# Later steps for the coefficient checks beside attention and for a layer's first normalisations

## The chip, the cores and the metric

The kernel runs on one core of a Trainium2 chip. The metric is the device time of one execution in microseconds (us), lower is better. A core has five engines that work side by side and wait for each other through semaphores: TensorE (PE, matmuls; its weight loads are listed apart as PEld), VectorE (DVE), ScalarE (ACT), GpSimd (POOL) and SyncE (SP), which here issues nearly all transfers between memory and the core. Each engine takes its own instructions strictly in the order in which they were put into its queue. So an instruction that waits holds up everything behind it on that engine, also what would be ready.

## The reference

Two blocks alternate, A B A B, on a sequence of 2048 rows of 512 numbers, each with a layer norm ahead and a residual sum behind. B's weights are the same both times.

```python
def _A_ref(x, dft_seq_re, dft_seq_im, dft_hid_re, dft_hid_im):
    a = jnp.einsum("bsd,ed->bse", x, dft_hid_re)
    b = jnp.einsum("bsd,ed->bse", x, dft_hid_im)
    return jnp.einsum("ts,bse->bte", dft_seq_re, a) - jnp.einsum("ts,bse->bte", dft_seq_im, b)

def _B_ref(x, wq, wk, wv, wo, beta):          # 32 heads of 16, 4 segments of 512 rows
    for s in range(N):
        logits = jnp.einsum("bhqd,bhkd->bhqk", qs, ks) * scale + mask
        a_dot = jnp.einsum("bhqk,bhkd->bhqd", _softmax(logits), vs)
        a_mem = (phi(qs) @ M) / (phi(qs) @ z + 1e-6)
        outs.append(g * a_mem + (1.0 - g) * a_dot)
        M = M + phi(ks).T @ vs; z = z + phi(ks).sum()
    return o @ wo

x = x + _A_ref(_layernorm(x), ...); x = x + _B_ref(_layernorm(x), ...)
x = x + _A_ref(_layernorm(x), ...); x = x + _B_ref(_layernorm(x), ...)
```

## The kernel before, in words

**Two layers.** A layer is a block A, here computed with far fewer matmuls than the reference, and a block B. Block A folds the sequence: rows that a Fourier matrix treats alike up to sign are added or subtracted first, so that a quarter of the matrix is left (`place_folded`). The 2048 rows come as eight octants; `A` and `B` in the code name four of them that belong to the first two segments of the attention before, `C` two of the third, `D` two of the fourth. For each half `k` (0 and 1) of the octants, the generator `fold(k)` goes through steps: load A and B; patch single edge rows (`edge`); normalise A and B (`normalise(k, "AB")`: four statistics on VectorE, one power on GpSimd, some small operations, four scalings on ScalarE); load C, patch it, normalise it; form sums and differences; take in D; fold again. The tile of A and B, `hAB`, lies in the buffer in which attention keeps the transposed rows `xT`, so it can be filled once the fourth segment's projections are done. After the folds, `contract` runs the matmuls with the Fourier coefficients.

**The checks.** Folding is only right if the Fourier matrices that are passed in have the symmetry that it uses. So the kernel reads both whole matrices and checks them, and falls back to a plain program if the check fails. There are 68 check units (`place_checks`), each a transfer of 512 KB into a tile `chk` and one or four ScalarE instructions that form the absolute differences and their sum (L900). Units 0 to 33 belong to the first layer and 34 to 67 to the second. Of each 34, the first 20 run beside the folds and the contraction, and the other 14 beside attention, one every 15 steps from step 85 of the attention on.

**Attention.** There are 4 segments x 4 groups x 2 = 32 units a layer, each of four heads, and a unit starts every ten steps. In its ten steps TensorE computes transposed scores `sT`, one piece a step; ScalarE clears what the mask forbids and takes the exponential into a probability tile `pT` (L1171, L1172); two steps behind the ten, a block of 32 matmuls (`pv_bank`) multiplies the probabilities with the values, and ScalarE copies the result to `ot` (L1245). Beside this run, for later units, the row maxima on VectorE (`nat`, `junk`, L1098), and for other segments projections, transposes, memory and output projection. The last two groups of the fourth segment apply the mask with a matmul, so there ScalarE has no clearing and GpSimd no selecting to do.

**Buffers.** Tiles with the same tag share a ring of buffers. The tag `wd` has eight buffers of 4 KB a partition. In attention they hold the `pT` tiles (four a unit), the `onat` tiles (two a segment; the next segment's two are taken 13 steps ahead of it, while the last segment's are in use until its rows are transposed) and `chk`. A buffer is held from the first write, for `chk` the transfer, to the last read.

**Order.** Every piece of work is a generator that is stepped at numbered slots, called steps here: `place(order, gen, slots)`. At the end all slots are gone through in order, and what is traced earlier has a higher priority. A planner then forms each engine's queue from the priorities, its own costs and the buffers that are free; matmuls keep the traced order (`in_order`), other instructions need not. `tc.high_priority` moves a few still further ahead. The numbers of the steps are written by hand: `a1 = 0`, `b1 = a1 + FOLD` with `FOLD = 56`, `LB = 320` steps of an attention, `a2 = b1 + LB + 20`, `b2 = a2 + FOLD`, and `e = b1 + LB` is the step at which the first layer's attention ends.

**The lines that the change touches.** `fold_at(k)`, the `lambda` in the second `place_folded`, gives `fold(k)` its ten steps. `check_at(k)` gives each check two steps: the first issues its transfer (L895), the second its ScalarE instructions (L900):

```python
if n < early:
    t = (a1, a2)[k // per] + 6 + 18 * n // early
else:
    t = (b1, b2)[k // per] + SPREAD + 15 * (n - early)
return [t, t + 3]
```

with `per = 34`, `early = 20`, `SPREAD = 85` and `n = k % per`.

Of the kernel before, what the change touches and what calls it, by code (L numbers as in the profile page):

```python
# [58 lines left out]
def spectral_infini_kernel(  # L59
# [60 lines left out]
    def rows(ap, i):  # L120
        return ap[i * P : (i + 1) * P, :]

    def bank(name, shape=(P, 512), dtype=F32):
        return psum.tile(list(shape), dtype, name=name, tag="bank", bufs=7)
# [4 lines left out]
    def load_rows(src, name="xt"):  # L129
        t = sb.tile([P, 512], F32, name=name, tag="xt", bufs=4)  # L130
        nc.sync.dma_start(t, src)
        return t
# [67 lines left out]
    def place(order, gen, *at):  # L200
        for t in itertools.chain(*at):
            slots.setdefault(t, []).append((order, gen))
# [1316 lines left out]
    if folded is None:  # L1519
        x_tiles = [rows(x, i) for i in range(NT)]  # L1520
        mids = [
            [dram.tile([P, D], F32, name=f"mid{n}_{i}") for i in range(NT)] for n in range(4)
        ]

        def w_at(b):
            return lambda k: b - 52 + 2 * k if k < 12 else b - 14 + 2 * (k - 12)

        a1 = 0
        b1 = a1 + 240 + LEAD
        a2 = b1 + LB + 30  # L1530
        b2 = a2 + 240 + LEAD
        place_spectral(x_tiles, mids[0], a1, lambda i: a1 - 6 + 2 * i - (30 if i == 0 else 0))
        place_attention(Plain(mids[0]), Plain(mids[1]), b1, {}, w_at(b1), lambda k: b1 + LB + 8 + k // 2)
        place_spectral(mids[1], mids[2], a2, lambda i: a2 - 6 + 2 * i)
        place_attention(Plain(mids[2]), Plain(mids[3]), b2, {}, w_at(b2), lambda k: b2 + LB + 8 + k)

        def turn_rows(i):
            t = load_rows(mids[3][i])
            yield
            home = Rows(out)  # L1540
            if i % LT >= 2:
                flip = sb.tile([P, P], F32, name="flip", tag="junk", bufs=1)
                G.memset(flip, 0.0)
                G.affine_select(
                    flip, flip, pattern=[[1, P]], compare_op=ALU.not_equal, fill=1.0, base=-P, channel_multiplier=1
                )
                G.memset(flip[0:1, 0:1], 1.0)
                ps = bank("turned")
                T.matmul(ps, flip, t, start=True, stop=True)
                t = sb.tile([P, 512], F32, name="turned", tag="xt", bufs=4)  # L1550
                A.activation(t, ps, AF.Copy)
            home.store(t, i // LT, i % LT)
            yield

        for i in range(NT):
            place(9, turn_rows(i), [b2 + LB + 40 + 2 * i, b2 + LB + 41 + 2 * i])
        setup_at = [60, 60]
    else:
        mids = [
            Rows(dram.tile([S, D], F32, name=f"mid{n}")) for n in range(3)  # L1560
        ]
        a1 = 0
        b1 = a1 + FOLD
        a2 = b1 + LB + 20
        b2 = a2 + FOLD
        ws = {}
        taken = []
        folded.flip = consts.tile([P, P], F32, name="flip")
        folded.masks = [consts.tile([P, 1], F32, name=f"edge{n}") for n in range(2)]
        for t, (edge, other) in zip(folded.masks, ((0.0, 1.0), (0.0, -1.0))):  # L1570
            V.memset(t, other)
            V.memset(t[0:1], edge)
        place_folded(
            Rows(x), mids[0], a1,
            [a1 - 12, a1 - 9, a1 - 6, a1 - 3, a1 - 1, a1 + 1, a1 + 4],
            folds=folded.folds,
        )
        place_attention(
            mids[0], mids[1], b1, ws, lambda k: a1 + 14 + k if k < 12 else b1 + 20 + 4 * (k - 12), lambda k: b1 + LB + 8 + k // 2,
            last=lambda *a: taken[0](*a), turned=True,  # L1580
        )
        e = b1 + LB
        place_folded(
            mids[1], mids[2], a2,
            lambda k: [e - 56 + 6 * k, e - 52 + 6 * k, e - 46 + 6 * k, e - 16 + 14 * k, e - 13 + 13 * k, e - 10 + 13 * k, e + 1 + 4 * k, *((e + 11, e + 13, e + 14) if k == 0 else (e + 15, e + 15, e + 17))],
            late=taken,
        )
        place_attention(
            mids[2], Rows(out), b2, ws, None, lambda k: b2 + LB + 8 + k, final=True, turned=True,
        )  # L1590
        SPREAD = 85
        per = (len(folded.checks) + 1) // 2

        def check_at(k):
            early = 20
            n = k % per
            if k < 8:
                return [a1 - 2 + k // 2, a1 + 6 + k // 3]
            if n < early:
                t = (a1, a2)[k // per] + 6 + 18 * n // early  # L1600
            else:
                t = (b1, b2)[k // per] + SPREAD + 15 * (n - early)
            return [t, t + 3]

        place(7, place_checks(check_at)(), [b2 + SPREAD + 220])
        setup_at = [a1 - 12, a1 + 6]

# [189 lines left out]
```

## Time and profile before

| | |
|---|---|
| median of 3 runs | 1250.4 us (1244.46 to 1254.6) |
| the profiled execution | 1249.04 us; span 1247.3 us from the first to the last instruction |
| mean granted TensorE clock | 0.983 |
| busy: PE, DVE, ACT, POOL | 1151.6, 963.2, 850.0, 443.0 us |
| first layer's attention, from the first copy of a value bank to the last | 163.4 to 620.5 us |
| the same in the second layer | 772.2 to 1232.6 us |

The rows of the profile that follow are copied as they stand. A group of instructions reads: line, engine, operation, tiles written and read, shapes, count, then busy us and mean ns of one, then the idle time of the engine just before them and what ended most of it. A piece of the chain of waits is a start and a length in us and what the end of the execution waited for in that time. A busy TensorE is not TensorE at its peak: the ends of matmuls are modelled in this profile, so that a matmul that stands still for a moment can look long rather than late.

### The profile page before, as it was taken

To read this page: it belongs to the slowest core of one execution; us is meant where nothing else is said; L and a number is where in the kernel's file an instruction comes from. 1 tells how busy PE (TensorE), PEld (TensorE's weight loads), DVE (VectorE), ACT (ScalarE), POOL (GpSimd) and SP (SyncE) were. 2 spreads that over 40 slices of the span, in tenths; PEclk is the share of its full clock that TensorE was granted. 3 is DMA by queue.
4 is the path that set the end of the run, shared out by engine and by line. 5 is a ranking of instruction groups with operands and counts; after the bars stand their busy time and mean duration, and the time that the engine had idled before them with its cause. 6 is when DMAs were issued, how large, how long until landed. Compare 5 with 4: busy or idle time off the path is not lost.

```text
span 1247.3 us, 24570 instructions
## 1 busy us (share of the span) xinstructions
PE 1151.6 (92%) x7720; PEld 743.9 (60%) x7720; DVE 963.2 (77%) x3560; ACT 850.0 (68%) x1928; POOL 443.0 (36%) x774
## 2 busy tenths in 40 slices
PE   6989898999999999988899998899999999999897
PEld 5767454666655665544577764556666566655454
DVE  8788887787877877777696798867787878767772
ACT  5463487887787787786525426788777887778762
POOL 1122453443444444441110244454434444435200
PEclk9999999999999999999999999999999999999999
DMA  9586544435544454462428773543354444534411
GB/s 364 182 299 222 183 138 132 126 120 165 161 152 119 146 172 138 125 220 88 169 71 278 257 243 119 162 127 122 123 177 156 134 127 153 166 128 130 148 45 54
DMA packets 111126, 197.67 MB, mean 158 GB/s; under 512 B 13917, under 2 KB 63075, under 8 KB 110986
## 3 DMA queue, kind: packets, MB, share of 16 engines
q1 hardware_dynamic: 107722, 195.22, 48.4%
q8 instruction: 63, 1.03, 0.3%
q10 hardware_dynamic: 3264, 0.79, 0.3%
q14 instruction: 77, 0.63, 0.2%
HBM read 128.04 MB, written 67.14 MB: 156 GB/s over the span
## 4 chain that ended last, share of the span: by engine, by line
PE 63%; DVE 14%; ACT 8%; DMA 6%; issue 5%; POOL 2%; SPq 0%; ACTq 0%; DVEq 0%; POOLq 0%
PE pqk L85 10%; PE pv_bank L85 10%; PE sT L85 8%; PE nat L85 8%; DVE junk L1098 7%; PE u L85 6%; PE pvv L85 6%; PE po L85 6%; DMA chk<-in_chk 3%; ACT pT L1172 3%; PE pm L85 2%; PE pM L85 2%; PE yr L85 2%; ACT sT L1171 2%; PE on L85 1%
## 5 line engine op out<-in xcount | busy, mean ns | idle before, releaser
L1098 DVE CUSTOM_DVE_ANT_0 junk<-nat,mask 128x512 bf16<-128x512 f32 (+3 forms) x1024 | 500.5, 489 | 146.3 <-PE nat L85 112.6
L1172 ACT ACTIVATE pT<-sT 128x512 f32<-128x512 f32 x640 | 367.6, 598 | 45.5 <-PE sT L85 20.3
L1177 POOL TENSOR_SCALAR_AFFINE_SELECT pT<-pT 128x512 f32<-128x512 f32 x392 | 170.5, 448 | 405.5 <-ACT pT L1172 363.9
L85 PE MATMUL sT<-stkq,stkk 99*128 99x256 bf16 (+3 forms) x1024 | 249.3, 306 | 14.7 <-DVE mx L1098 7.8
L85 PE MATMUL nat<-stkk,stkq 96*128 96x512 bf16 (+3 forms) x1024 | 236.9, 303 | 16.7 <-DVE mx L1098 15.1
L1171 ACT ACTIVATE sT<-sT 128x256 f32<-128x256 f32 (+1 forms) x560 | 182.0, 334 | 49.5 <-PE sT L85 46.4
L85 PEld LDWEIGHTS <-stkk 99*128 99x128 bf16 x1024 | 82.8, 99 | 135.9 <-issue 121.6
L85 PE MATMUL pv_bank<-pT,vt 128*17 128x128 f32 (+3 forms) x2048 | 152.8, 435 | 0.0
L85 PEld LDWEIGHTS <-stkq 96*128 96x128 bf16 x1024 | 92.8, 99 | 65.1 <-issue 29.5
L85 PE MATMUL pqk<-xT,wq 128*128 128x512 f32 x384 | 127.3, 444 | 3.8 <-ACT xT L100 2.2
L85 PE MATMUL pvv<-wv,xT 128*128 128x512 f32 x384 | 125.8, 442 | 2.1 <-DVE mx L1098 2.1
L85 PE MATMUL pqk<-xT,wk 128*128 128x512 f32 x384 | 124.7, 436 | 1.2 <-ACT pT L1172 0.5
L85 PE MATMUL po<-wo,oh 128*128 128x512 f32 x384 | 121.2, 432 | 2.7 <-DVE oh L102 1.9
L900 ACT ACTIVATE chk<-chk,reps 128x1024 f32<-128x1024 f32 (+1 forms) x80 | 81.3, 1021 | 39.3 <-DMA chk<-in_chk 38.7
L85 PEld LDWEIGHTS pv_bank<-pT,vt 128*17 128x17 f32 x2048 | 53.7, 97 | 80.5 <-issue 75.3
L1282 POOL TENSOR_TENSOR onat<-onat,otmp 128x128 f32<-128x128 f32 x96 | 48.6, 514 | 105.2 <-DVE otmp L1281 102.1
L1098 DVE DVE_READ_ACCUMULATOR2_ANT mx<- 128x1 f32 x1024 | 84.5, 82 | 0.0
L1038 POOL TENSOR_TENSOR parts<-rem,parts 128x512 bf16<-128x512 f32 x60 | 71.8, 1196 | 27.8 <-ACT parts L1034 24.2
L85 PEld LDWEIGHTS po<-wo,oh 128*128 128x128 f32 x384 | 67.6, 191 | 22.4 <-DVE oh L102 4.8
L85 PEld LDWEIGHTS pqk<-xT,wq 128*128 128x128 f32 x384 | 69.5, 192 | 17.0 <-ACT xT L100 2.6
L85 PEld LDWEIGHTS pvv<-wv,xT 128*128 128x128 f32 x384 | 69.4, 195 | 16.1 <-DVE mx L1098 4.2
L85 PEld LDWEIGHTS pqk<-xT,wk 128*128 128x128 f32 x384 | 67.6, 191 | 14.1 <-issue 0.9
(255 smaller groups left out, 1700.4 us busy)
## 6 DMA issues: line engine op xcount, KB each, us to landing
chk<-in_chk SPq DMA_DIRECT2D x68, 512.0 KB
stkq<-scrq SPq DMA_DIRECT2D x64, 384.0 KB
stkk<-scrk SPq DMA_DIRECT2D x64, 384.0 KB
scrq<-parts SPq DMA_DIRECT2D x32, 384.0 KB
scrk<-parts SPq DMA_DIRECT2D x32, 384.0 KB
mid<-xrm SPq DMA_DIRECT2D x32, 256.0 KB
scrq<-parts SPq DMA_DIRECT2D x32, 256.0 KB
scrk<-parts SPq DMA_DIRECT2D x32, 256.0 KB
```

Of the source, the lines that this page charges most:

```text
L85: return tc.keep_in_program_order(op(*args, **kwargs))
L900: A.activation(t[:, c : c + row], t[:, c : c + row], AF.Abs, bias=rep[:, col : col + 1], scale=scale, accum_out=acc[:, col : col + 1],)
L1038: E.tensor_tensor(out=parts[:, 2], in0=rem, in1=parts[:, 1], op=ALU.subtract)
L1098: V.tensor_tensor_reduce(junk[:, :n], src, mask[:, 512 - n :], 1.0, 3e38, ALU.add, ALU.min, dst,)
L1171: A.activation(blocks, blocks, AF.Relu)
L1172: A.activation(dst, ps, AF.Exp, scale=-SCALE)
L1177: G.affine_select(blocks, blocks, pattern=[[0, n] for n in blocks.shape[1:-1]] + [[1, P]], compare_op=ALU.is_ge, fill=0.0, base=0, channel ...
L1282: G.tensor_tensor(out=dst, in0=dst, in1=tmp, op=ALU.add)
```

## The change

The ScalarE part of the 28 checks beside attention is traced nine steps behind its transfer, not three; the transfer keeps its step. The checks beside the folds, and the first eight of all, are as they were.

In the folds for the second layer, which start while the first layer's attention still runs, the first three steps of both halves are later: loading A and B from `e - 56` (k = 0) and `e - 50` (k = 1) to `e - 38` and `e - 32`; the edge rows from `e - 52` and `e - 46` to `e - 34` and `e - 28`; normalising A and B from `e - 46` and `e - 40` to `e - 25` and `e - 17`. That is 18, 18 and 21 steps for the first half and 18, 18 and 23 for the second. Everything from the load of C on keeps its step.

```diff
             mids[1], mids[2], a2,
-            lambda k: [e - 56 + 6 * k, e - 52 + 6 * k, e - 46 + 6 * k, e - 16 + 14 * k, e - 13 + 13 * k, e - 10 + 13 * k, e + 1 + 4 * k, *((e + 11, e + 13, e + 14) if k == 0 else (e + 15, e + 15, e + 17))],
+            lambda k: [e - 38 + 6 * k, e - 34 + 6 * k, e - 25 + 8 * k, e - 16 + 14 * k, e - 13 + 13 * k, e - 10 + 13 * k, e + 1 + 4 * k, *((e + 11, e + 13, e + 14) if k == 0 else (e + 15, e + 15, e + 17))],
             late=taken,
...
             else:
                 t = (b1, b2)[k // per] + SPREAD + 15 * (n - early)
+                return [t, t + 9]
             return [t, t + 3]
```

## The prediction

> **What bounds the kernel now.** I read the profile's page first, then what the scalar engine (ACT) waited for, then the chain of waits, and last single stretches. On the page:
>
> ```profile
> PE 1151.6 (92%) x7720; PEld 743.9 (60%) x7720; DVE 963.2 (77%) x3560; ACT 850.0 (68%) x1928; POOL 443.0 (36%) x774
> PE 63%; DVE 14%; ACT 8%; DMA 6%; issue 5%; POOL 2%; SPq 0%; ACTq 0%; DVEq 0%; POOLq 0%
> L900 ACT ACTIVATE chk<-chk,reps 128x1024 f32<-128x1024 f32 (+1 forms) x80 | 81.3, 1021 | 39.3 <-DMA chk<-in_chk 38.7
> ```
>
> TensorE is busiest and holds most of the chain, but the attention is a loop over engines that wait for each other, and 38.7 us of ACT's idle time ended with a check's data landing. Not all of that is touched: only the 28 checks that run beside attention (14 in each layer) move, and not those beside the folds. So I asked for ACT's waits in the attention of the first layer (260 to 600 us), of the second (870 to 1190 us), and, for a price used below, over the whole run:
>
> ```profile
> ACT chk L900 <- DMA chk<-in_chk: 7.1, 5, 2.1
> ACT chk L900 <- DMA chk<-in_chk: 7.4, 5, 2.1
> ACT pT L1172 <- PE pv_bank L85: 11.5, 12, 1.4
> ```
>
> The columns are us in total, times, longest. The checks that move hold 7.1 + 7.4 = 14.5 us of waiting, in ten of 28 cases. The chain of waits (start, us, what) has six of them on it, at the loads below; the last row is the block of value matmuls that closes each ten-step unit.
>
> ```profile
> 293.26 5.63 DMA chk<-in_chk
> 388.75 4.92 DMA chk<-in_chk
> 481.62 5.02 DMA chk<-in_chk
> 996.95 4.06 DMA chk<-in_chk
> 1087.72 6.52 DMA chk<-in_chk
> 1177.97 5.12 DMA chk<-in_chk
> 343.13 2.28 PE pv_bank L85 x32
> ```
>
> A load lands 4.06 to 6.52 us after its issue; three steps are about that long. But the 4 to 6 us pieces are not the price: ACT worked through most of them. Its timeline (start, us, instruction, idle before it in brackets) gives what it really stood still, and for one further check that the chain does not hold:
>
> ```profile
> 298.92 1.15 ACT L900 ACTIVATE chk<-chk,reps 128x1024 f32<-128x1024 f32 x1 [1.25 <-DMA chk<-in_chk]
> 393.69 1.15 ACT L900 ACTIVATE chk<-chk,reps 128x1024 f32<-128x1024 f32 x1 [1.20 <-DMA chk<-in_chk]
> 486.67 1.15 ACT L900 ACTIVATE chk<-chk,reps 128x1024 f32<-128x1024 f32 x1 [1.79 <-DMA chk<-in_chk]
> 1001.03 1.15 ACT L900 ACTIVATE chk<-chk,reps 128x1024 f32<-128x1024 f32 x1 [0.34 <-DMA chk<-in_chk]
> 1094.26 1.15 ACT L900 ACTIVATE chk<-chk,reps 128x1024 f32<-128x1024 f32 x1 [2.10 <-DMA chk<-in_chk]
> 1183.12 0.51 ACT L900 ACTIVATE chk<-chk,reps 128x256 f32<-128x256 f32 x1 [2.06 <-DMA chk<-in_chk]
> 345.86 1.15 ACT L900 ACTIVATE chk<-chk,reps 128x1024 f32<-128x1024 f32 x1 [2.13 <-DMA chk<-in_chk]
> 906.44 1.14 ACT L900 ACTIVATE chk<-chk,reps 128x1024 f32<-128x1024 f32 x1
> ```
>
> The six on the chain add up to 1.25 + 1.20 + 1.79 + 0.34 + 2.10 + 2.06 = 8.74 us. The other 14.5 - 8.74 = 5.8 us lie off it; the one at 345.86 shows why. The value block runs from 343.13 to 345.41, ACT's next piece is the copy of that bank, and so 1.68 of its 2.13 us were idle anyway.
>
> **The checks, part by part.** The two layers run the same steps, so they are an experiment already made. Below are the same two units of either layer, cut where ACT copies the value bank (columns: stretch and length, then busy time and instructions of PE, PEld, DVE, ACT, POOL, the granted clock, DMA).
>
> ```profile
> 296.24:314.33 18.09, 16.85 (x122) 11.47 (x122) 15.64 (x60) 12.12 (x28) 3.79 (x9) 1.00 0.60 196
> 905.09:922.57 17.48, 17.00 (x122) 11.44 (x123) 15.87 (x60) 12.06 (x29) 3.82 (x9) 1.00 0.56 185
> 390.08:405.33 15.25, 14.05 (x98) 8.54 (x97) 10.48 (x48) 10.97 (x27) 3.89 (x9) 1.00 0.42 113
> 998.28:1012.69 14.41, 14.07 (x98) 8.55 (x97) 10.48 (x48) 10.96 (x27) 3.89 (x9) 1.00 0.39 117
> ```
>
> The first pair has the check with a wait of 1.25 and with none, and differs by 0.61; the second has 1.20 and 0.34 and differs by 0.84. So 1.45 us of time for 2.11 us of waiting: 0.69. Six steps more are 8.6 us at the least (a unit of ten steps took 14.41 to 18.09 us), against a wait of 2.13 at most: all ten waits go. On the chain that is 8.74 x 0.69 = 6.0 us; off it I count nothing, with up to 5.8 x 0.69 = 4.0 as the other end.
>
> The check's own work stays, at another place. On the six spots its 1.15 us came right behind the wait, with the exponentials queued behind it and, behind them, the value matmuls. Six steps on it costs nothing if ACT is free there, and the same 1.15 us if not: 0 to 6 x 1.15 = 6.9 us gained. ACT is free for (17.48 - 12.06)/17.48 = 31% of such a unit, so I take 0.31 x 6.9 = 2.1. The other 22 checks move as well; having cost no time that I can see, they could cost up to as much again: -2.1 is the end I keep. The loads themselves keep their step, so SP's queue does not change for them. The buffer that a check holds is held six steps longer; that is the first rival.
>
> [...]
>
> **The folds.** What moves: in each of two turns, four loads of 256 KB and the small edge rows (SP), four statistics with their aggregates and small steps (DVE), one power (POOL) and four scalings (ACT). The next rows are the costs by group (busy and mean ns, then idle before), the first statistic and a late scaling, and the stretches of the units: two in the first layer, the same two in the second, which has no folds, and the two at the new place.
>
> ```profile
> L430 ACT ACTIVATE hAB<-hAB,nb,rr 128x512 f32<-128x512 f32 x8 | 6.0, 819 | 4.0 <-DVE nb L425 4.0
> L408 DVE BATCH_NORM_STATS2 st<-hAB 128x6 f32<-128x512 f32 x8 | 5.4, 679 | 2.2 <-DMA hAB<-mid 2.2
> 545.62 0.70 DVE L408 BATCH_NORM_STATS2 st<-hAB 128x6 f32<-128x512 f32 x1 [2.18 <-DMA hAB<-mid]
> 574.05 0.81 ACT L430 ACTIVATE hAB<-hAB,nb,rr 128x512 f32<-128x512 f32 x1 [3.99 <-DVE nb L425]
> 545.71:560.85 15.14, 12.01 (x87) 6.42 (x86) 14.67 (x63) 11.31 (x32) 4.50 (x11) 1.00 0.88 293
> 560.85:579.76 18.91, 14.89 (x106) 8.54 (x106) 14.92 (x70) 13.89 (x30) 4.70 (x10) 1.00 0.30 93
> 1154.97:1167.83 12.86, 11.47 (x87) 6.45 (x86) 10.96 (x47) 11.01 (x31) 3.86 (x10) 1.00 0.59 183
> 1167.83:1184.12 16.29, 13.45 (x106) 8.12 (x106) 12.28 (x52) 9.69 (x25) 3.19 (x8) 1.00 0.39 115
> 592.22:603.40 11.18, 9.99 (x93) 6.10 (x94) 9.45 (x39) 6.34 (x12) 0.91 (x2) 1.00 0.41 134
> 603.40:612.06 8.66, 7.72 (x77) 4.50 (x76) 4.17 (x16) 6.58 (x14) 0.87 (x2) 1.00 0.56 198
> ```
>
> At the old place DVE is busy 14.67 of 15.14 us, DMA 0.88, and ACT stands 3.99 us behind a DVE that is late. The two units take 34.05 us against 29.15 in the second layer, although the second holds the 2.06 us wait of 1183.12: the folds cost 4.9 to 7.0 us there. Units end 12 steps behind their first, so the new steps, 25 and 17 ahead of the layer's end, fall into the last two stretches. There DVE is idle for 19.84 - 13.62 = 6.2 us and ACT for 6.9: room for 5.4 and 6.0 us, but tight, and the scalings come as blocks of four ahead of exponentials. New cost: between 0 and 6.0 us; half, 3.0, since each engine has just the room. POOL, with two powers to run, is idle there. SP issues eight loads, between the stack loads, in a stretch with less traffic.
>
> But a later step is not a later instruction. The first statistic ran at 545.62, at the end of a unit that closes at step 262 of the layer, with its step at 274: the planner fills an engine's holes with whatever has its data. Loads and statistics may stay; the scalings, behind exponentials of the new steps, will not. So of the 4.9 to 7.0 I take 5. Net 5 - 3 = 2 us gained; ends: 7.0 gained, 6.0 lost.
>
> Sum: 6.0 + 2.1 + 2.0 = 10.1 us off the profiled execution's 1249.04 (span 1247.3), so **1239**. The median of the runs shown is 1250.4, 1.4 above that execution and inside their spread of 1244.46 to 1254.6, so I leave it uncorrected.
>
> **Rivals.** *The ring of buffers runs dry (slower).* The check shares eight buffers with the probability tiles, four a unit, and with the output tiles, two a segment and four while two segments overlap. 4 + 4 + 1 = 9: in those steps (7 of 14 checks a layer by the code's steps) a check held nine steps leaves the next exponential without a buffer. If that waits out a value block, 2.28 us, then 14 x 2.28 = 32 us come in against 10 out: 1271. It makes the kernel slower by over 1% from 1.6 us each. For it: the 11.5 us that exponentials wait for the value matmuls now, 0.96 each in 12 cases. Against it: a planner that sees the buffer missing can put the check forward, which costs its order alone, and its data are there.
>
> *Nothing moves that matters.* The planner fills holes with checks as it does with statistics, or the waits lie under TensorE's work as at 345.86: 1249. [...] The unit pairs above (0.69) speak against it.
>
> *More than the sum.* If every wait counts in full and the folds cost nothing at their new place: 14.5 + 7.0 = 21.5 off, 1227.5. For it: the second pair, 0.84 for 0.86. Against: 345.86.
>
> **Chances.** Forecast 0.59 (its own range 1233 to 1245), more 0.17, nothing 0.17, ring 0.07. A measurement of this kernel tells about 1% from no change, 12.5 us: below 1237.9 or above 1262.9. Some 0.42 of the forecast's own range lies below 1237.9, so faster 0.59 x 0.42 + 0.17 = 0.42; slower 0.06 (the ring, most of it); same 0.52. The range, 1228 to 1250, takes in the second and third case to their prices and leaves out the ring and half of the case above the sum.
>
> **What would show it.** Right: ACT's waits for checks in the two attentions fall from 14.5 to under 2 us; a check runs 9 us or more behind its load; the units of 18.09 and 15.25 us shorten to 17.5 and 14.4; the two units of 34.05 us come down towards 29 to 30, and the two of 19.84 grow by up to 3. Wrong: checks still three or four steps behind their loads (nothing moves); more than 11.5 us of exponentials behind the value matmuls (ring); the last two units growing by 6, or the first matmul of the second layer's folds waiting for the scaled tile (folds too late); or the chain passing from checks to another wait of equal length in the same units.

## The result and the profile after

The changed kernel takes 1256.46 us in the median of 14 runs (1249.59 to 1268.07), the kernel before 1249.71 us in 14 runs beside them (1244.46 to 1256.24). The ratio is 1.0054 with a 95% interval of 1.0031 to 1.0077: about 6.7 us slower, where 10 us less were forecast. The profiled execution took 1257.36 us, with a span of 1255.6 against 1247.3.

The page of the changed kernel, in the same lines that the prediction shows of the kernel before: the engines' busy time, the chain's shares, the group of the checks.

```profile
PE 1157.9 (92%) x7720; PEld 747.2 (60%) x7720; DVE 965.3 (77%) x3560; ACT 853.2 (68%) x1928; POOL 441.8 (35%) x774
PE 34%; DVE 10%; ACT 3%; DMA 3%; issue 3%; POOL 1%; ACTq 0%; SPq 0%; DVEq 0%; POOLq 0%
L900 ACT ACTIVATE chk<-chk,reps 128x1024 f32<-128x1024 f32 (+1 forms) x80 | 81.2, 1017 | 39.0 <-DMA chk<-in_chk 38.6
```

The last line says it at once: 38.6 us of idle time before checks, 38.7 before. (The shares of the chain add up to 54% of the span, against 98% before, so they aren't compared.) The waits of ACT in the attention of the first layer (260 to 607 us) and of the second (871 to 1199 us), then the waits of exponentials over the whole run and those of TensorE's value matmuls (us in total, times, longest):

```profile
ACT chk L900 <- DMA chk<-in_chk: 7.0, 4, 3.1
ACT chk L900 <- DMA chk<-in_chk: 7.0, 6, 2.1
ACT pT L1172 <- PE pv_bank L85: 9.6, 8, 1.9
```

```profile
PE pv_bank L85 <- POOL pT L1177: 2.8, 2, 1.8
```

14.0 us in ten waits stand where 14.5 us in ten stood. Exponentials wait less for the value matmuls than before (9.6 against 11.5). New is the last line: value matmuls that wait for probabilities, of which the trace of before has none.

**The checks stayed where they were.** ACT works its queue in order (in the last section a copy whose bank was done at 488.04 runs at 491.89, behind a check that waited for 3.15 us), so a place in it can be counted: how many exponentials of the layer ran before each of the 14 checks. (The last two checks of a layer are four instructions each; the first is counted.) The counts are the same in both layers.

```
check of the layer        1    2    3    4    5    6    7    8    9   10   11   12   13   14
before                   88  103  119  133  149  165  178  193  209  223  238  254  268  283
after                    88  103  122  133  149  165  178  193  209  223  238  254  268  283
```

The second step is six later, and only the third check stands elsewhere. Two things did move. Where a check was traced ahead of other work of the same moment, it is now behind it. Here is the first check of the first layer, in ACT's timeline, before and then after; `vt<-pvv` is a copy that waits for a projection.

```profile
268.33 0.59 ACT L1172 ACTIVATE pT<-sT 128x512 f32<-128x512 f32 x1
268.81 1.15 ACT L900 ACTIVATE chk<-chk,reps 128x1024 f32<-128x1024 f32 x1
...
271.09 0.62 ACT L990 ACTIVATE vt<-pvv 128x512 f32<-128x512 f32 x1
```

```profile
269.81 0.59 ACT L1172 ACTIVATE pT<-sT 128x512 f32<-128x512 f32 x1
271.25 0.26 ACT L1171 ACTIVATE sT<-sT 128x128 f32<-128x128 f32 x1 [0.84 <-PE sT L85]
272.15 0.60 ACT L990 ACTIVATE vt<-pvv 128x512 f32<-128x512 f32 x1 [0.65 <-PE pvv L85]
272.65 1.14 ACT L900 ACTIVATE chk<-chk,reps 128x1024 f32<-128x1024 f32 x1
273.78 0.37 ACT L1171 ACTIVATE sT<-sT 128x256 f32<-128x256 f32 x1
274.08 1.55 ACT L1172 ACTIVATE pT<-sT 128x512 f32<-128x512 f32 x3
```

Before, the check filled the time in which ACT had nothing to do. After, ACT stands idle for 0.84 and 0.65 us, and then the check's 1.15 us come ahead of work that is ready. The unit, before and after (stretch and length, busy time and instructions of PE, PEld, DVE, ACT, POOL, clock, DMA):

```profile
262.42:275.99 13.57, 13.57 (x98) 8.39 (x97) 10.43 (x48) 10.84 (x27) 2.99 (x7) 1.00 0.43 128
```

```profile
263.90:278.06 14.16, 14.02 (x98) 8.94 (x97) 10.65 (x48) 10.94 (x27) 2.98 (x7) 1.00 0.42 123
```

0.59 us are lost; the same unit of the second layer also goes from 13.57 to 14.16.

**The divided checks came apart.** The last two of a layer are four instructions of 256 columns. Before, they stood together. In the second layer after, they lie between exponentials, which are left out of this timeline of ACT; TensorE's value matmuls of the same unit follow, with the windows of the unit and of 3.4 us in it.

```profile
1167.69 0.50 ACT L900 ACTIVATE chk<-chk,reps 128x256 f32<-128x256 f32 x1
...
1170.98 0.51 ACT L900 ACTIVATE chk<-chk,reps 128x256 f32<-128x256 f32 x1
...
1171.47 0.51 ACT L900 ACTIVATE chk<-chk,reps 128x256 f32<-128x256 f32 x1
...
1172.21 1.08 ACT L1172 ACTIVATE pT<-sT 128x512 f32<-128x512 f32 x2
1173.18 0.51 ACT L900 ACTIVATE chk<-chk,reps 128x256 f32<-128x256 f32 x1
```

```profile
1171.07 1.04 PE L85 MATMUL pv_bank<-pT,vt 128*17 128x512 f32 x4
1173.87 4.03 PE L85 MATMUL pv_bank<-pT,vt 128*17 128x512 f32 x28 [1.77 <-POOL pT L1177]
```

```profile
1160.83:1177.95 17.12, 14.35 (x87) 7.20 (x86) 11.54 (x50) 11.40 (x32) 3.85 (x10) 0.90 0.45 139
1174.10:1177.50 3.40, 3.40 (x27) 1.33 (x20) 0.21 (x2) 0.60 (x1) 0.00 (x0) 0.50 0.01 2
```

Two pieces run ahead of two exponentials. GpSimd gets their probability tiles late, the value block breaks off after 4 of 32 matmuls and waits 1.77 us, and then TensorE runs for 3.4 us at a granted clock of 0.50, so by estimate, half of 3.4, another 1.7 us go. The unit takes 17.12 us, against 12.86 before.

### The profile page after: what moved, and what is told of

It is laid out like the page before. It is cut to its first block, busy times and chain, and to the rows that moved or that the text cites. A ratio compares the mean times of both kernels' runs of the same rounds, so it can differ in the third digit from the quotient of the medians.

```text
span 1255.6 us, 24575 instructions
## 1 busy us (share of the span) xinstructions
PE 1157.9 (92%) x7720; PEld 747.2 (60%) x7720; DVE 965.3 (77%) x3560; ACT 853.2 (68%) x1928; POOL 441.8 (35%) x774
## 4 chain that ended last, share of the span: by engine, by line
PE 34%; DVE 10%; ACT 3%; DMA 3%; issue 3%; POOL 1%; ACTq 0%; SPq 0%; DVEq 0%; POOLq 0%
PE pv_bank L85 6%; PE sT L85 5%; PE pqk L85 5%; DVE junk L1098 5%; PE nat L85 4%; PE u L85 4%; PE po L85 4%; PE pvv L85 2%; DMA chk<-in_chk 1%; PE pm L85 1%; ACT pT L1172 1%; PE on L85 1%; PE pM L85 1%; DMA mid<-xrm 1%; DMA hC<-mid 1%
## 5 line engine op out<-in xcount | busy, mean ns | idle before, releaser
L1177 POOL TENSOR_SCALAR_AFFINE_SELECT pT<-pT 128x512 f32<-128x512 f32 (+1 forms) x392 | 169.1, 445 | 418.0 <-ACT pT L1172 370.5
L85 PE MATMUL pv_bank<-pT,vt 128*17 128x128 f32 (+3 forms) x2048 | 158.6, 442 | 2.8 <-POOL pT L1177 2.8
L85 PEld LDWEIGHTS pv_bank<-pT,vt 128*17 128x17 f32 x2048 | 56.6, 98 | 85.9 <-issue 75.0
L900 ACT ACTIVATE chk<-chk,reps 128x1024 f32<-128x1024 f32 (+1 forms) x80 | 81.2, 1017 | 39.0 <-DMA chk<-in_chk 38.6
L85 PEld LDWEIGHTS pvv<-wv,xT 128*128 128x128 f32 x384 | 68.6, 192 | 15.5 <-DVE mx L1098 4.5
```

The costliest lines, as they stand in the source:

```text
L85: return tc.keep_in_program_order(op(*args, **kwargs))
L900: A.activation(t[:, c : c + row], t[:, c : c + row], AF.Abs, bias=rep[:, col : col + 1], scale=scale, accum_out=acc[:, col : col + 1],)
L1177: G.affine_select(blocks, blocks, pattern=[[0, n] for n in blocks.shape[1:-1]] + [[1, P]], compare_op=ALU.is_ge, fill=0.0, base=0, channel ...
```

## The experiments

The theory after the result: a step in the code is a priority and not a place in the queue; the planner runs a check as soon as ACT has a hole and it counts on the data; so the waits stay, and the loss is disorder that the lower priority makes. The rivals: the folds' part lost what the checks won; or the checks' waits are worth nothing at all; or the ring of eight buffers took the gain. All ratios are to the kernel before, which ran beside each.

**One half of the change each.** Only the second hunk of the diff (`return [t, t + 9]`), and only the first (`fold(k)`'s steps).

> Only the check part of the change: the 28 checks traced nine steps behind their loads, the folds as before. The theory of the prediction (the waits go): 6 to 8 us faster than before, ratio 0.994 to 0.995, ACT's waits for checks in the two attentions under 2 us. The theory of the planner (a step is a priority, and ScalarE's queue takes a check as soon as its data are counted on; in the built queue 25 of the 28 stand where they stood, only the third check of each layer moves by 3 exponentials and the last two, of four pieces each, come apart between exponentials): waits still 12 to 16 us, and slower by the whole of the change's loss, ratio 1.003 to 1.007, most of it in the unit with the pieces of the second layer's last but one check.

> Only the fold part of the change, the checks as before. The theory of the prediction: 2 us faster (7 faster to 6 slower). The theory of the planner: loads and statistics stay at 545 to 570 us, the eight scalings come apart over exponentials 275 to 293 rather than in two blocks, and nothing else moves: ratio 0.998 to 1.002. If the folds carry the loss, 1.003 to 1.007.

Measured: the checks alone 1.0047 (1.0014 to 1.0080), the folds alone 1.0000 (0.9970 to 1.0029). The checks' part carries the loss. The folds' part is worth nothing that can be measured, either way.

**Which checks.** The ninth step for the last two checks of a layer only (`if n >= 32: return [t, t + 9]`), and for the other twelve only (`if n < 32`).

> Only the last two checks of each layer's attention, the ones that ScalarE does as four instructions of 256 columns, get the ninth step; the other 24 and the folds are as before. Theory A (the loss of the change is these four checks, whose pieces come apart between exponentials): 1.003 to 1.006 of the time before, as the check part alone gave 1.0047, and value matmuls of the second layer's unit at 1160 us wait for GpSimd as in the changed kernel. Theory B (the loss is the third check of each layer, which goes three exponentials back, and what shifts in the planner's other queues): 1.000 to 1.001.

> The other half: the 24 undivided checks get the ninth step, the last two of each layer keep three; the folds are as before. In the built queue only the third check of each layer stands elsewhere (behind 122 exponentials and not 119). Theory A: 0.999 to 1.001 of the time before. Theory B: 1.003 to 1.006. If both runs lie near 1.002, each half carries a part.

Measured: 1.0029 (1.0000 to 1.0058) and 1.0033 (1.0004 to 1.0061). Neither theory alone; each half carries 3.6 to 4.1 us in the mean, with intervals that reach down to nothing. The traces keep them apart: the unit of the first check and the unit of the divided check in the second layer, in the run of the divided checks and then in the run of the others:

```profile
264.36:277.93 13.57, 13.57 (x98) 8.40 (x97) 10.41 (x48) 10.84 (x27) 2.99 (x7) 1.00 0.41 128
1156.03:1171.45 15.42, 12.64 (x87) 6.72 (x86) 11.54 (x50) 11.38 (x32) 3.85 (x10) 1.00 0.47 152
```

```profile
263.27:277.44 14.17, 14.03 (x98) 8.94 (x97) 10.71 (x48) 10.94 (x27) 2.99 (x7) 1.00 0.40 123
1157.94:1170.81 12.87, 11.49 (x87) 6.45 (x86) 10.97 (x47) 11.01 (x31) 3.87 (x10) 1.00 0.57 186
```

The pieces cost 15.42 - 12.86 = 2.56 us in their unit, of which the next two units of the layer give back 1.5. The undivided checks cost 0.6 us where the first one stands, in each layer. The rest of the 4 us is spread over units that differ from run to run by as much, and isn't placed.

**Nine steps in fact.** As the check part, and each check now ordered behind the exponential that is traced before it, so that it can't run earlier:

```diff
-                A.activation(dst, ps, AF.Exp, scale=-SCALE)
+                exps.append(A.activation(dst, ps, AF.Exp, scale=-SCALE))
...
-                with after((opened, drained[:1], drained[1:2])[min(k // 2, 2)] if k < 20 else ()):
+                with after((opened, drained[:1], drained[1:2])[min(k // 2, 2)] if k < 20 else exps[-1:] if k % 34 >= 20 else ()):
```

> The checks as the steps say: nine steps behind their loads, and in ScalarE's queue tied behind the exponential of that step, so that the planner cannot put them forward (in the queue they stand 6 to 8 exponentials later than before). The folds as before. If the waits are worth 0.69 of their length and the check's own work is hidden in part: all ten waits gone, 6 to 8 us faster, ratio 0.994 to 0.995. If the waits lie under TensorE's work and cost nothing: 0.999 to 1.001. If the buffer held longer costs a value block in 14 checks: up to 30 us slower, ratio 1.01 to 1.025.

Measured: 1.0125 (1.0093 to 1.0156), 15.6 us slower. The checks now stand behind 95, 110, 125, 140 ... exponentials, and none in attention waits for its data. What came in their place, in the waits of ACT and of TensorE over the run:

```profile
ACT pT L1172 <- PE pv_bank L85: 32.4, 27, 1.8
```

```profile
PE pv_bank L85 <- POOL pT L1177: 17.7, 10, 1.9
```

Exponentials wait 21 us more for the value matmuls to free a buffer, and then ten value blocks wait for late probabilities, 1.77 us in the mean.

**The same with a buffer of its own.** The checks beside attention take a tile of their own; to make room, the ring of row tiles `xt` has two buffers, not four.

```diff
-            t = pair("chk", *(("w", 16) if leads else ("wd", 8)), F32)
+            t = pair("chk", *(("w", 16) if leads else ("wd", 8) if k % 34 < 20 else ("own_chk", 1)), F32)
```

> The nine steps as in the run where all checks are tied that late, but with a buffer of their own for the checks beside attention (4 KB a partition, paid for by two buffers less for rows that are loaded, four to two). If the loss there is the ring of eight buffers: no value matmul waits for a probability tile, and against that run 16 us and the worth of the waits come back: ratio to before 0.985 to 0.997, unless the two row buffers cost time of their own. If the loss is the checks' place among the exponentials: 1.008 to 1.015 again.

> The same buffer of their own for the checks, with the steps of before (three) and nothing tied, as the partner of the run above: both have two row buffers less. In the built queues the planner now takes a layer's 14 checks one behind the other from step 70 to 153 rather than one every 15 steps from 88 to 283. If the ring of buffers was what kept a check at its step, and waits for data cost 0.69 of their length, the waits stay (a load goes out when the buffer comes free, and ScalarE is made to wait for it): ratio 0.995 to 1.005. If two row buffers are too few: above 1.01 here and in the partner.

Measured: nine steps in fact 0.9983 (0.9952 to 1.0014); `t + 3` and no order 0.9958 (0.9930 to 0.9985). With nine steps and the buffer of their own, no value block waits for late probabilities, and the 32.4 us of waiting exponentials fall to this:

```profile
ACT pT L1172 <- PE pv_bank L85: 4.6, 5, 1.0
```

All but two of the 14 checks of a layer stand behind as many exponentials as without that buffer. So the ring was what the late checks paid for: 1.0125 to 0.9983 is 18 us. The second run isn't a clean one: free of the ring, the planner put a layer's 14 checks between the 70th and the 153rd exponential. Why the first stays behind the 0.9928 below isn't settled: the halved ring of row tiles and the places of the checks both differ.

**What the checks cost in all.** One run leaves out the 28 checks beside attention, transfer and ScalarE work (the answer of those checks isn't formed); one keeps the 28 transfers and leaves out their ScalarE work.

> Leaves out the 28 checks beside attention, transfer and ScalarE work both (so these parts of the matrices are not checked). It bounds what any place of these checks can win. If the waits and the check's own work lie on the path as the prediction has it, 6 + 6.9 us and more: ratio 0.985 to 0.99. If they lie under other work: 0.997 to 1.000.

> Keeps the 28 transfers beside attention and leaves out the ScalarE work of these checks (so these parts are loaded and not checked). Leaving out both took 15.6 us off. If that was the ScalarE work and its waits: the same again, ratio 0.985 to 0.990. If it was the transfers' traffic or the buffers that they hold: 0.995 to 1.000.

Measured: 0.9875 (0.9846 to 0.9904) and 0.9883 (0.9840 to 0.9926). The two can't be told apart, so the transfers cost nothing that shows; ScalarE's part, waits and work, is worth some 15 us.

**Only the checks that wait, and only as far as the ring allows.** The even checks of a layer (second, fourth ...: `k % 2`) are the ones that wait: their step falls at the start of a unit, so that their load is issued just as it begins. Only they get a later step and the order behind its exponential; the others are as before.

```diff
-                with after((opened, drained[:1], drained[1:2])[min(k // 2, 2)] if k < 20 else ()):
+                with after((opened, drained[:1], drained[1:2])[min(k // 2, 2)] if k < 20 else exps[-1:] if k % 34 >= 20 and k % 2 else ()):
...
+                if k % 2:
+                    return [t, t + 6]
```

> Of the 14 checks a layer beside attention, only the seven whose load is issued as a unit starts (all ten waits are theirs) go later, to six steps, tied behind the exponential of that step. By the code's steps they are done before a unit needs its fourth probability buffer. If the waits cost 0.69 of their length on the chain and the loss of the nine steps was the buffer: no check waits, value matmuls wait for no probability tile, 6 to 10 us faster than before, ratio 0.992 to 0.995. If a check among the exponentials costs what its wait cost: 0.999 to 1.002. If holding the buffer longer costs in any place: above 1.003.

> As the run with seven checks a layer tied behind the exponential of the sixth step after the load, but of the fifth: in the built queue three exponentials further back than before, not four. A step is 1.4 to 1.8 us and the waits removed were 0.3 to 2.1 us, so both remove all or nearly all of the waits. Theory that the waits are what that run gained: 0.990 to 0.996 here too, waits for check data in the attentions under 2 us. Theory that the gain came from where the check falls in the unit (its 1.15 us in ScalarE's free time): a different ratio, 0.996 or more or 0.988 or less, with the same waits.

Measured: six steps 0.9928 (0.9892 to 0.9965), five steps 0.9929 (0.9897 to 0.9962). In both, no check of the attention waits for its data; they stand behind 107, 137, 167 ... (six) or 106, 136, 166 ... (five) exponentials, where they stood behind 103, 133, 165. That the two agree speaks for the waits as what was gained, not for a lucky place. Exponentials behind the value matmuls stay at what they were (11.5 us before; the run with six steps):

```profile
ACT pT L1172 <- PE pv_bank L85: 12.0, 11, 1.6
```

The units of 18.09 and 15.25 us of the prediction, there, and one of its checks:

```profile
299.34:316.24 16.90, 16.65 (x122) 11.43 (x122) 15.45 (x60) 12.11 (x28) 4.10 (x9) 1.00 0.56 181
390.88:404.94 14.06, 13.80 (x98) 8.38 (x97) 10.41 (x48) 10.86 (x26) 3.81 (x9) 1.00 0.45 125
```

```profile
305.90 1.14 ACT L900 ACTIVATE chk<-chk,reps 128x1024 f32<-128x1024 f32 x1
```

They lose 1.19 us each. No idle time stands ahead of the check: its data are there at its turn.

**That, with the folds of the change.**

> The run in which seven checks a layer stand four exponentials further back (0.9928) and the later folds of the change together. Theory that the folds' new steps are worth nothing either way: 0.990 to 0.996. Theory that they cost where the scalings now stand among exponentials and checks: 0.997 or more. Theory of the prediction (two units come down by 5, the last two grow by 3): 0.989 to 0.992.

Measured: 0.9907 (0.9876 to 0.9937), 1238.21 us against 1249.68. Its ratio is the lowest of the complete kernels, below the kernel before and the changed one; from the runs with six or five steps alone it can't be told apart. The folds add 0.2%, less than the intervals can tell from nothing.

## Why the prediction was wrong

**The step that failed** is the first sentence on the moved checks: "Six steps more are 8.6 us at the least ... all ten waits go." It takes a step for a place in ACT's queue. In the trace 26 of 28 checks kept their count of exponentials (the expectation of the first run says 25), and the waits went from 14.5 to 14.0 us. That the planner counts on the data too early is inferred from these places; no run changes what it counts on. The prediction had the rule itself, further down, for the folds ("a later step is not a later instruction"), and had seen a statistic run twelve steps early. Had it used the same reading on the checks, the rival "nothing moves" would have been the forecast. The trace of before had it too: every check was traced three steps behind its load, yet two exponentials ran between the load at 293.26 and its check, and six between the next check's load (313.09) and its ScalarE work (323.12).

**The price was about right.** 6.0 us for the waits and 2.1 for the work, 8.1 together. With the seven waiting checks of each layer really moved, the gain is 0.72% of 1250 us, 9.0 us (4.4 to 13.5). With the folds, 11.6 us (7.9 to 15.5) against the sum of 10.1, and 1238.2 against 1239. The sum priced an edit that the changed kernel isn't. No run tests the 6.0 and the 2.1 apart, and the intervals are wide, so that the agreement to a microsecond is partly luck.

**What the 22 others cost.** The end kept for them was -2.1 us. With no gain from the waits, the checks' part as a whole costs 5.9 us (1.8 to 10.0). Two causes were not in the prediction: the pieces of the divided checks come apart (their rows in the trace of before show four instructions together, and nothing bound them), and a check with lower priority goes behind a copy that waits.

**The ring** was told right as a mechanism and wrong as a rival to this change. It needs a check that is held nine steps; here only the third was held some exponentials longer, and the pieces of the divided ones. The prediction's own counter ("a planner that sees the buffer missing can put the check forward") points to the cause in part: the check already stood ahead of its step in the kernel before. Where checks were held in fact, the price was asked: 14 x 2.28 = 32 us in against 10 out, 1271; measured 1266.2, with waits of 17.7 us on TensorE.

**Nothing moves that matters** (1249) was the nearest of the cases, right for the waits and 7 us short of the time, since "nothing" included the order that got worse. Its second reason, that the waits lie under TensorE's work, is wrong for most of them: taken away, they give 9 us, and in the changed kernel TensorE stands still for copies that ACT has queued behind a waiting check (2.94, 1.81 and 1.82 us; the last section has the rows).

**The folds.** The loads didn't move: the first was issued 5.48 us before the end of its unit (540.23 against 545.71) and is now issued 5.45 us before (546.75 against 552.20). The first statistic moved by 0.27 us against that end. The scalings, of which the prediction said that they would not stay, didn't go later as blocks: they were pulled apart. The first stood 3.05 us behind the end of its unit (563.90 against 560.85) and now stands 0.50 behind it (570.54 against 570.04); only the last is far behind. Before and after, in ACT's timeline:

```profile
563.90 2.93 ACT L430 ACTIVATE hAB<-hAB,nb,rr 128x512 f32<-128x512 f32 x4
574.05 0.81 ACT L430 ACTIVATE hAB<-hAB,nb,rr 128x512 f32<-128x512 f32 x1 [3.99 <-DVE nb L425]
576.20 2.22 ACT L430 ACTIVATE hAB<-hAB,nb,rr 128x512 f32<-128x512 f32 x3
```

```profile
570.54 0.80 ACT L430 ACTIVATE hAB<-hAB,nb,rr 128x512 f32<-128x512 f32 x1
...
582.55 1.51 ACT L430 ACTIVATE hAB<-hAB,nb,rr 128x512 f32<-128x512 f32 x2
584.55 0.80 ACT L430 ACTIVATE hAB<-hAB,nb,rr 128x512 f32<-128x512 f32 x1
596.10 0.82 ACT L430 ACTIVATE hAB<-hAB,nb,rr 128x512 f32<-128x512 f32 x1
```

The units, of 34.05 and 19.84 us before. First the two at the old place in the changed kernel, then these two and the two at the new place in the run with the folds alone:

```profile
552.20:570.04 17.84, 13.16 (x87) 6.66 (x86) 16.15 (x73) 11.42 (x31) 4.92 (x11) 1.00 0.78 261
570.04:585.74 15.70, 13.08 (x101) 7.70 (x102) 13.18 (x60) 13.69 (x29) 4.21 (x9) 1.00 0.29 89
```

```profile
557.62:572.79 15.17, 11.98 (x87) 6.41 (x86) 14.71 (x63) 11.31 (x31) 4.48 (x11) 1.00 0.89 292
572.79:589.35 16.56, 13.58 (x101) 7.92 (x102) 14.22 (x69) 12.92 (x28) 4.69 (x10) 1.00 0.28 92
601.78:612.96 11.18, 9.99 (x93) 6.11 (x94) 9.44 (x39) 6.34 (x13) 0.91 (x2) 1.00 0.40 134
612.96:621.48 8.52, 7.71 (x77) 4.49 (x76) 4.06 (x16) 6.57 (x13) 0.87 (x2) 1.00 0.55 202
```

The changed kernel's 33.54 us hold the pieces of a divided check too: its first unit takes 17.61 us in the run with the ninth step for the divided checks alone, against 15.14 before. With the folds alone the units take 31.73 and 19.70, in one execution and at a granted clock of 1.00 as before: 2.3 us down, all in the second unit, and not 5; and none of the 3 up. (The prediction calls the new place the last two units; one more, of 8.42 us, follows.) The term "of the 4.9 to 7.0 I take 5" took the cost of that stretch for the scalings'; loads and statistics stayed, and so did more than half of the cost. That the two differences come near the net of 2.0 is luck, since both terms were too large. Over the whole run the net measured 0.0 (3.8 us gained to 3.6 lost), which neither shows nor excludes it.

**What the prediction left out of a wait's price** is the clock. In the changed kernel the granted clock was 0.50 for 6.9 us behind one wait (the last section has the rows); the measured gain of 9 us doesn't come from it.

## What to carry to other kernels

Where a planner orders the queues, a number in the code is a wish: before pricing a move, look in the trace how far instructions stand from the numbers that they have now, and if they already run early, tie them to an instruction instead. A wait on a transfer is taken away at the few instructions that show it; moving all of their kind also moves those that stood well, and work in several pieces falls apart when its priority falls. Hold a shared buffer no longer than the wait needs: the seven waiting checks of a layer two to four exponentials later gained 9 us, all fourteen six to eight later cost 16.

## What the runs showed of the hardware

In the changed kernel a stop of TensorE of 2.94 us comes with a granted clock of 0.50 for 6.9 us. The tenth check of the first layer waits for 3.15 us, the copy of the value bank is behind it on ACT (the bank's last matmul ended at 488.04), and TensorE waits for the copy. ACT's timeline, TensorE's timeline, and two windows:

```profile
490.74 1.15 ACT L900 ACTIVATE chk<-chk,reps 128x1024 f32<-128x1024 f32 x1 [3.15 <-DMA chk<-in_chk]
491.80 0.19 ACT L900 ACTIVATION_READ_ACCUMULATOR chk<-chk,reps 128x1 f32 x1
491.89 0.58 ACT L1245 ACTIVATE ot<-pv_bank 128x512 f32<-128x512 f32 x1
```

```profile
492.52 1.12 PE L85 MATMUL on<-ident,ot 128*128 128x128 f32 x4 [2.94 <-ACT ot L1245]
```

```profile
491.40:494.80 3.40, 2.28 (x10) 1.96 (x11) 0.53 (x4) 3.30 (x9) 0.76 (x2) 0.51 0.05 17
494.80:498.30 3.50, 3.50 (x13) 2.24 (x11) 1.73 (x9) 2.30 (x6) 1.64 (x4) 0.50 0.00 0
```

The granted clock falls to 0.5 at 491.4, while TensorE still stands, and stays there for 6.9 us. TensorE is busy for 5.8 us of that. Three `pvv` matmuls (128x512) take 1.73 us there, at 494.03, against 0.95 us at 488.18 with a clock of 1.00. So by estimate, half of the 5.8, 2.9 us of full speed are lost beside the stop itself. After the stop of 1.77 us that ends at 1173.87 the clock was 0.50 for 3.4 us. What makes it fall and what ends it, no run shows.

Of two stops of nearly the same length one came with a low clock and one did not. TensorE's timeline of the changed kernel has them; both end with a copy behind a waiting check:

```profile
1101.97 0.73 PE L85 MATMUL on<-ident,ot 128*128 128x128 f32 x4 [1.81 <-ACT ot L1245]
1194.96 0.66 PE L85 MATMUL on<-ident,ot 128*128 128x128 f32 x4 [1.82 <-ACT ot L1245]
```

From 1102.4 to 1105.8 the granted clock was 0.50; from 1195.0 to 1198.4 it was 1.00. So single units of two profiles can't be compared to a microsecond unless their clock stands beside them.

Over whole runs of the kernel before the time goes with the clock as well: in the 29 runs beside the run with five steps their correlation is -0.88. The one with the lowest mean clock, 0.970, was the longest, 1261.11 us, and the one with the highest, 0.990, the shortest, 1242.87 us. But the gain of 9 us isn't clock. The runs with six and five steps had a mean clock of 0.980 and 0.979, the runs of before beside them 0.981 and 0.979, and in the mean they took 9.1 and 8.8 us less. It comes from the waits and the place of the checks' work, with whatever shifts in the other queues; how it divides, no run shows. Nor is the loss clock: the checks' part alone took 6.1 us more at a mean clock of 0.980 on both sides.
